# The first block of the second phase: transposed on TensorE instead of by a DMA, its rows gathered before its shares, and the renewal of two weight pieces set behind the fetch

## The chip, the cores and the metric

The kernel runs on one core of a Trainium2 chip. The metric is the time of one execution in device microseconds (us). Three executions of the kernel before took 579.71 us in the median. The profile is of one more execution.

## The reference

A linear attention (softmax of q over the head dimension, softmax of k over the sequence) feeds a mixture of eight experts, in which every token takes exactly one expert. A token takes the expert of its highest logit, or, where its local gate is 0.5 or more, the expert of the token before it.

```python
kv = np.einsum('bhsd,bhse->bhde', k_s, v)
x = np.einsum('bhsd,bhde->bhse', q_s, kv)        # 8 batches, 8 heads, 576 tokens, 64 -> rows of 512
...
for b in range(B):
    prev_e = -1
    for s in range(S):
        fresh_e = int(np.argmax(logits[b, s]))
        if s == 0 or local_gate[b, s] < 0.5:
            e = fresh_e
        else:
            e = prev_e if prev_e >= 0 else fresh_e
        prev_e = e
        ...
        h = np.maximum(x[b, s] @ w1[e], 0.0)     # 512 x 1024
        out[b, s] = p[e] * (h @ w2[e])           # 1024 x 512
```

## The kernel before

**The work.** The attention part writes the 4608 rows of x to DRAM (`xrows`) and each row's share p[e] to `shares`. The expert part then works through blocks of 128 rows of one expert. Blocks 0 to 7 are the first phase: they hold rows of the first four batches and run while the attention of the other four is still being finished. From block 8 on (`NP`, `NA` = 8) the index lists cover all rows; that is the second phase. With the inputs used, the reference's rule sends blocks 0 to 8 to expert 0, 9 to 13 to expert 2, 14 to 18 to expert 4, 19 to 23 to expert 5 and 24 to 37 to expert 7; so the weights change four times, before blocks 9, 14, 19 and 24.

**One block.** Each step has a name, and a number for the block:

- `G` (POOL) gathers the 128 rows into `xg`, four blocks ahead; `Gp` (POOL) gathers their 128 shares into `pb`.
- `Px` normalises the rows (`xn`; POOL, for blocks 8 and 10 VectorE), `Ph` makes their fp16 high part and `Pl` the low part (`x2`; ACT or DVE, and DVE).
- The rows are turned so that the 512 features lie on the partitions (`xT`). Block 0 does it with `T`, eight TensorE transposes into PSUM, and `Tc`, a VectorE copy out of it. All other blocks use `D`, a DMA transpose that SP issues.
- `F1` (PE, two halves, `.0` and `.1`) multiplies with w1 into PSUM (`ph`, `pi`); `Ac`, `Ad`, `Ar`, `Al` (ACT, DVE, ACT, DVE) make the fp16 high and low parts of the hidden values (`hi`, `lo`) of a half; `F2` (PE, two halves) multiplies with w2 (`py`, `pq`); `Gv` (ACT) scales by the share and `Pt` (POOL) scatters the rows to the output.

**The weights.** `fetch(b, 1)` and `fetch(b, 2)` are two DMAs that SP issues on a condition: they load the 2 MB of the next expert's w1 into the staging tile `s1`, of its w2 into `s2`, if block b is the first of its expert. `renew` cuts staged weights into fp16 high and low parts, in 16 pieces (0 to 7 of w1, 8 to 15 of w2), each a step on ACT and one on DVE, inside an `If` on the flag that the block begins an expert. `RN` and `s1`, `s2` are the names of these steps in the first phase.

**What sets the order.** For the attention part and blocks 0 to 7, and for the preparation of blocks 8 to 10, a text (`ORDER`) lists all steps by name; each engine runs its own steps in that order, and waits only for what a step needs. From block 8 on, `block(b)` writes the steps. Its renewals for the block after it end with pieces 8 and 9.

**The place of the change.** The stretch of `ORDER` around the end of block 7 is, on PE: `F2.7.0`, then the first step of `block(8)`, `F1.8.0` (`ffn1`, line 869, `hidden`, lines 888 and 893), then `F2.7.1` and `F1.8.1`. On SP: `s1.7` (the w1 of expert 2), `s2.7`, `s1.8`, and then `D.8`, `D.9`, `D.10` (`turn_dma`, line 866). `s1.8` may not write `s1` before the fetch of `s1.7` has landed there; its condition is false in this run, so it moves nothing. On DVE: `Px.8`, `Ph.8`, `Pl.8` (lines 845, 191, 853), `Ad.7.1` (901), `Px.10`, `Al.7.1` (908), `Pl.9`, `Ph.10`, `Pl.10`.

Of the kernel before, what the change touches and what calls it, by code (L numbers as in the profile page):

```python
# [18 lines left out]
B, H, S, D = 8, 8, 576, 64  # L19
# [12 lines left out]
NA = 8  # L32
NB = NBM - NA
NP = 8
NQE = 3
NT_PE = 1
NW = 6
NG = NE + 1
NX = 1 + NG + D
# [14 lines left out]
class Plan:  # L54
# [7 lines left out]
    def add(self, name, eng, fn, after=(), takes=(), uses=(), order=(), alt=None):  # L62


        eng = alt if name in self.swap else eng
        before = list(order) + list(uses)
        for r, _ in takes:
            if r in self.chained:
                before += [self.head[r]] if r in self.head else []
                self.head[r] = name  # L70
        self.tasks[name] = (eng, fn, list(after), list(takes), before, alt)
        for u in takes:
            self.taker[u] = name
        for u in set(uses) | set(takes):
            self.users.setdefault(u, []).append(name)
# [68 lines left out]
ro.2.0 Al.4.0 RN.4.3 bc Gv.3 s2.4 ro.3.4 bi.p0 Gp.7 bi F2.4.0 Ac.4.1 Pt.3 RN.5.1 bj.p0 ro.3.8 s1.5 Ad.4.1 ro.3.0 bj.p1 F1.5.0 RN.5.2 Ar.4.1 bj.p2  # L144
ro.3.1 Al.4.1 bj.p3 ro.3.7 F2.4.1 bj.p4 Ac.5.0 RN.6.0 Ad.5.0 ro.3.3 bj Ar.5.0 F1.5.1 bb.p0 Gv.4 RN.5.3 Pt.4 ro.3.5 s2.5 Al.5.0 ro.3.6 ro.3.2 F2.5.0
RN.6.1 bb Ac.5.1 s1.6 bo.0 Ad.5.1 bo.3 Ar.5.1 bo.1 bm.0 RN.6.2 Al.5.1 bm.1 bm.3 bo.2 F1.6.0 F2.5.1 Ac.6.0 RN.7.0 Ad.6.0 Ar.6.0 Al.6.0 F1.6.1 Gv.5
RN.6.3 Pt.5 s2.6 bm.2 Ac.6.1 F2.6.0 bx.p0 RN.7.1 s1.7 Ad.6.1 bx Ar.6.1 Gp.8 Al.6.1 F1.7.0 RN.7.2 G.8 G.9 F2.6.1 RN.8.0 Ac.7.0 G.10 Ad.7.0 G.11 Ar.7.0
F1.7.1 Al.7.0 Gv.6 RN.7.3 Px.8 Pt.6 s2.7 Ph.8 Px.9 F2.7.0 Ac.7.1 Pl.8 RN.8.1 Ph.9 s1.8 Ad.7.1 D.8 Px.10 Ar.7.1 Al.7.1 Pl.9 D.9 Ph.10 Pl.10 D.10
"""


# [1 line left out]
def moe_kernel(ctx, tc, q, k, v, w_gate, w_local, w1, w2, out, dbg=None):  # L153
# [23 lines left out]
    def at(pair, b):  # L177

        return pair[0][:, b] if b < NA else pair[1][:, b - NA]
# [647 lines left out]
    def word(w_, hi_, engines):  # L827
        return nc.values_load(w_, min_val=0, max_val=hi_, engines=engines,
                              skip_runtime_bounds_check_because="clamped where it is worked out")

    def gather(b):
        src = xrows[0:2 * 1152, :] if b < NA else xrows
        i_, j_ = (gidx[0], b) if b < NA else (gidx[1], b - NA)
        nc.gpsimd.indirect_dma_start(out=xg[b % AHEAD], out_offset=None, in_=src,  # L834
                                     in_offset=bass.IndirectOffsetOnAxis(ap=i_[:, j_:j_ + 1], axis=0))

    def gather_share(b):
        src = shares[0:2 * 1152, :] if b < NA else shares
        i_, j_ = (gidx[0], b) if b < NA else (gidx[1], b - NA)
        nc.gpsimd.indirect_dma_start(out=pb[b % NPB], out_offset=None, in_=src,  # L840
                                     in_offset=bass.IndirectOffsetOnAxis(ap=i_[:, j_:j_ + 1], axis=0))
# [121 lines left out]
    def renew(b, pieces):  # L963
        with tc.If(fst[b] == 1):  # L964
            for i in pieces:
                cut_hi(i, nc.scalar)
                cut_lo(i, nc.vector)
# [6 lines left out]
    def fetch(b, i):  # L974

        if b >= NBM - 1:
            return
        s_, src = ((W["s1"], w1_src), (W["s2"], w2_src))[i - 1]
        w_ = at(info, b)
        cond, e = w_[:, 4:5], w_[:, 1:2]  # L980
        if b == NA - 1:
            cond = None if i == 1 else w_[:, 0:1]
        elif b == NA - 2 and i == 2:
            cond, e = w_[:, 2:3], w_[:, 3:4]
        kw = {} if cond is None else dict(cond=(word(cond, 1, [ET.SP]) == 1), cond_hint=False)
        nc.sync.dma_start(out=s_, in_=src(bass.ds(word(e, NE - 1, [ET.SP]), 1)), **kw)
# [4 lines left out]
    add, split = pl.add, pl.split  # L991
    plan.append(pl)
    PE, DVE, ACT, POOL, SP = "PE", "DVE", "ACT", "Pool", "SP"
# [88 lines left out]
    for b in range(NP + 4):  # L1082
        add(("G", b), POOL, gather, after=[("ax",) if b < NA else ("bx",)] + [("xs", t, u) for t in range(2 if b < NA else NTILE) for u in range(3)],
            order=[("ow",)], takes=[("xg", b)])
        if b <= NP:
            add(("Gp", b), POOL, gather_share, after=[("ax",) if b < NA else ("bx",)] + [("Sd", t) for t in range(1 if b < NA else 2)],
                order=[("ow",)], takes=[("pb", b)])
        if b >= NP + 3:
            continue
        add(("Px", b), POOL, prep_x, alt=DVE, after=[("G", b)], uses=[("xg", b)], takes=[("xn", b)])  # L1090
        add(("Ph", b), ACT, prep_hi, alt=DVE, after=[("Px", b)], uses=[("xn", b)], takes=[("x2", b)])
        add(("Pl", b), DVE, prep_lo, after=[("Ph", b)], uses=[("xn", b), ("x2", b)])
        if b < NT_PE:
            add(("T", b), PE, turn, after=[("Pl", b)], takes=[("pst", b)], uses=[("x2", b)])
            add(("Tc", b), DVE, turn_copy, after=[("T", b)], uses=[("pst", b)], takes=[("xT", b)])
        else:
            add(("D", b), SP, turn_dma, after=[("Pl", b)], uses=[("x2", b)], takes=[("xT", b)])
        if b > NP:
            continue
        if b > 0:  # L1100
            for i in range(2 if b == NP else 4):
                src = [("F1", b - 1, 0), ("F1", b - 1, 1), ("F2", b - 1, 0), ("F2", b - 1, 1)][i]
                add(("RN", b, i), ACT, renew4, after=[src, ("aj",) if b < NA else ("bj",)], order=[("s1" if i < 2 else "s2", b - 1)])
            add(("s1", b), SP, lambda b: fetch(b, 1), after=[("RN", b, 1)] + ([("bj",)] if b >= NA - 1 else []))
        else:
            add(("s1", b), SP, lambda b: fetch(b, 1), after=[("Wl", i) for i in range(8)] + [("aj",)], order=[("W", 3)])
        if b == NP:
            continue
        add(("s2", b), SP, lambda b: fetch(b, 2),
            after=([("RN", b, 3)] if b else [("Wl", i) for i in range(8, 16)] + [("aj",)]) + ([("bj",)] if b >= NA - 2 else []))  # L1110
        for g in range(2):
            wp_ = [("Wl", 4 * g + i) for i in range(4)] if b == 0 else [("RN", b, g)]
            add(("F1", b, g), PE, ffn1, after=[("Tc" if b < NT_PE else "D", b)] + wp_, order=[("ow",)] + ([("F2", b - 1, g)] if b else [("F1", 0, 0)] * g)
                + ([("F1", b, 0)] if g else []), takes=[("psh", (b, g))], uses=[("xT", b)])
            add(("Ac", b, g), ACT, act_copy, after=[("F1", b, g)], uses=[("psh", (b, g))], takes=[("hf", (b, g))])
            add(("Ad", b, g), DVE, act_add, after=[("Ac", b, g)], uses=[("psh", (b, g)), ("hf", (b, g))])
            add(("Ar", b, g), ACT, act_hi, after=[("Ad", b, g)], uses=[("hf", (b, g))] + ([("hh", b)] if g else []), takes=[] if g else [("hh", b)])
            add(("Al", b, g), DVE, act_lo, after=[("Ar", b, g)], uses=[("hf", (b, g)), ("hh", b)])
            if b == NP - 1 and g:
                continue  # L1120
            wp_ = [("Wl", 8 + 4 * g + i) for i in range(4)] if b == 0 else [("RN", b, 2 + g)]
            add(("F2", b, g), PE, ffn2, after=[("Al", b, g)] + wp_, order=[("F1", b, 1)] if g == 0 else [("F1", b + 1, 0)],
                takes=[] if g else [("psy", b)], uses=[("hh", b)] + ([("psy", b)] if g else []))
        if b < NP - 1:
            add(("Gv", b), ACT, give, after=[("F2", b, 1), ("Gp", b)], uses=[("psy", b), ("pb", b)], takes=[("y", b)])
            add(("Pt", b), POOL, put, after=[("Gv", b)], uses=[("y", b)])
# [3 lines left out]
    def prep_a(b):  # L1130
        if b < NBM:
            prep_x(b)
# [12 lines left out]
    def next_(b, pieces):  # L1145
        if b + 1 < NBM:
            renew(b + 1, pieces)

    def block(b):


        if b + AHEAD < NBM:
            gather(b + AHEAD)
        prep_a(b + 3)
        if b + 1 < NBM:
            gather_share(b + 1)
            if b + 1 not in fst:
                flag(b + 1)
        ffn1(b, 0)
        act(b, 0)  # L1160
        renew(b, FROM[b][0])
        next_(b, (0, 1))
        ffn2(b - 1, 1)
        ffn1(b, 1)
        give(b - 1)
        put(b - 1)
        renew(b, FROM[b][1])
        next_(b, (2, 3))
        prep_b(b + 3)
        act(b, 1)  # L1170
        renew(b, FROM[b][2])
        next_(b, (4, 5, 6, 7))
        ffn2(b, 0)
        next_(b, (8, 9))
        if b + 3 < NBM:
            turn_dma(b + 3)
        fetch(b, 2)
        if b + 1 < NBM:
            fetch(b + 1, 1)


    FROM = {b: ((10, 11), (12, 13), (14, 15)) for b in range(NBM)}
# [50 lines left out]
```

## Time and profile before

| | |
|---|---|
| median of three executions | 579.71 us (576.01 to 580.80) |
| the profiled execution | 581.13 us |
| its span, first to last instruction | 579.4 us |
| TensorE busy, share of the span | 86% |
| mean granted TensorE clock, share of 2.4 GHz | 0.946 |

The span is 1.7 us shorter than the profiled execution's own time, and that execution is 1.4 us above the median. A sum made in the trace is therefore taken off 581.13 us, and then 1.4 us more are taken off to compare it with the median.

### The profile page before, as it was taken

What the parts mean: (1) busy time and instruction counts of PE and PEld (TensorE: products, weight loads), DVE (VectorE), ACT (ScalarE), POOL (GpSimd) and SP (SyncE); (2) the same over time, 40 slices, a digit from 0 to 9 for tenths busy, and PEclk for the clock granted to TensorE, in tenths of its full rate; (3) what the DMA queues carried; (4) which work ended last, traced back from release to release, by engine and by line L of the source; (5) the groups of instructions that cost most, each with busy time, mean ns of one, the idle gap of its engine ahead of it and who ended that gap; (6) DMA issues with size and microseconds to landing.
All of it is one profiled execution on the core that took longest, in us unless ns stands there. A gap on an engine that the chain in (4) does not pass through costs nothing. (4 is left out here: it accounts for less than half of the span.)

```text
span 579.4 us, 16087 instructions
## 1 busy us (share of the span) xinstructions
PE 500.4 (86%) x6074; PEld 353.1 (61%) x6074; DVE 344.3 (59%) x651; ACT 267.5 (46%) x454; POOL 231.1 (40%) x239
## 2 busy tenths in 40 slices
PE   1677677665799999859999899999998999999995
PEld 0556556554666767546666566766666667766762
DVE  5978999997775784428535833674386333333331
ACT  2625557566533283217335633654374333333332
POOL 3551528525345111514535335334445253352431
PEclk9877899986799999969999999999999999999999
DMA  9999695639546202934973794279559934242351
GB/s 307 384 381 384 219 307 202 230 125 359 181 89 155 58 20 48 381 79 115 302 109 99 203 213 104 75 207 207 105 106 297 115 94 82 61 116 61 82 95 48
DMA packets 80435, 98.59 MB, mean 170 GB/s; under 512 B 47679, under 2 KB 55871, under 8 KB 80320
## 3 DMA queue, kind: packets, MB, share of 16 engines
q1 hardware_dynamic: 72672, 74.92, 45.8%
q0 software_dynamic: 7648, 22.20, 14.4%
q8 instruction: 65, 1.06, 0.8%
q14 instruction: 50, 0.41, 0.3%
HBM read 206.76 MB, written 20.89 MB: 393 GB/s over the span
## 5 line engine op out<-in xcount | busy, mean ns | idle before, releaser
L926 POOL DMA_INDIRECT out<-y,sidx x38 | 39.0, 1027 | 201.0 <-ACTq L964 160.6
L888 PEld LDWEIGHTS <-w1h 128*128 128x128 f16 x1216 | 104.6, 99 | 15.4 <-issue 0.8
L888 PE MATMUL ph<-xT,w1h 128*128 128x256 f16 (+1 forms) x640 | 101.4, 272 | 11.5 <-DMA xT<-x 8.8
L893 PEld LDWEIGHTS <-w1l 128*128 128x128 f16 x1216 | 91.8, 98 | 26.5 <-issue 12.4
L919 PEld LDWEIGHTS <-hi 128*128 128x128 f16 x608 | 58.9, 98 | 61.8 <-ACT hi L904 6.2
L888 PE MATMUL pi<-xT,w1h 128*128 128x256 f16 (+1 forms) x576 | 89.2, 268 | 0.0
L908 DVE SCALAR_TENSOR_TENSOR lo<-hf,hi 128x512 f16<-128x512 f32 x76 | 55.3, 728 | 44.7 <-ACTq L964 36.5
L904 ACT ACTIVATE hi<-hf 128x512 f16<-128x512 f32 x76 | 47.8, 629 | 71.6 <-DVE hf L901 69.9
L901 DVE TENSOR_TENSOR hf<-ph,hf 128x512 f32<-128x512 f32 x40 | 27.6, 691 | 75.2 <-ACT hf L898 63.4
L919 PE MATMUL py<-w2h,lo 128*128 128x512 f16 x184 | 69.8, 379 | 1.6 <-DVEq L964 1.2
L919 PE MATMUL py<-w2h,hi 128*128 128x512 f16 x184 | 69.8, 379 | 1.4 <-ACT hi L904 1.4
L919 PE MATMUL py<-w2l,hi 128*128 128x512 f16 x184 | 69.7, 379 | 0.0
L898 ACT COPY hf<-ph 128x512 f32<-128x512 f32 x40 | 23.4, 584 | 93.0 <-PE ph L888 85.9
L893 PE MATMUL ph<-xT,w1l 128*128 128x128 f16 (+1 forms) x640 | 61.9, 219 | 0.5 <-issue 0.5
L853 DVE SCALAR_TENSOR_TENSOR x<-xn,x 128x512 f16<-128x512 f32 x41 | 34.6, 845 | 38.4 <-ACT x L187 36.9
L840 POOL DMA_INDIRECT pb<-shares,gidx x39 | 42.7, 1095 | 35.0 <-ACTq L964 12.5
L834 POOL DMA_INDIRECT xg<-xrows,gidx x42 | 47.1, 1121 | 21.1 <-issue 11.1
L919 PEld LDWEIGHTS <-lo 128*128 128x128 f16 x304 | 29.9, 98 | 41.3 <-DVE lo L908 3.5
L893 PE MATMUL pi<-xT,w1l 128*128 128x128 f16 (+1 forms) x576 | 54.4, 217 | 0.0
L919 PE MATMUL pq<-w2h,hi 128*128 128x512 f16 x120 | 46.3, 385 | 3.7 <-ACT hi L904 3.7
L919 PE MATMUL pq<-w2h,lo 128*128 128x512 f16 x120 | 46.1, 384 | 0.3
L919 PE MATMUL pq<-w2l,hi 128*128 128x512 f16 x120 | 46.2, 385 | 0.0
(227 smaller groups left out, 754.6 us busy)
## 6 DMA issues: line engine op xcount, KB each, us to landing
s<-in_moe_w SPq DMA_DIRECT2D x77, 2048.0 KB
xrows<-xt SPq DMA_DIRECT2D x12, 888.0 KB
KT<-in_k SPq DMA_DIRECT2D x16, 576.0 KB
VT<-in_v SPq DMA_DIRECT2D x16, 576.0 KB
qt<-in_q SPq DMA_DIRECT2D x8, 640.0 KB
qt<-in_q SPq DMA_DIRECT2D x8, 512.0 KB
s<-in_moe_w SPq DMA_DIRECT2D x4, 1024.0 KB
xg<-xrows,gidx POOLq DMA_INDIRECT x42
```

Source lines behind the costliest of these rows:

```text
L834: nc.gpsimd.indirect_dma_start(out=xg[b % AHEAD], out_offset=None, in_=src, in_offset=bass.IndirectOffsetOnAxis(ap=i_[:, j_:j_ + 1], axis=0))
L840: nc.gpsimd.indirect_dma_start(out=pb[b % NPB], out_offset=None, in_=src, in_offset=bass.IndirectOffsetOnAxis(ap=i_[:, j_:j_ + 1], axis=0))
L853: nc.vector.scalar_tensor_tensor(out=x2[b % 2][:, 1, :], in0=xn[b % 2], scalar=XS, in1=x2[b % 2][:, 0, :], op0=ALU.mult, op1=ALU.subtract)
L888: nc.tensor.matmul(ph_[:, f, :].rearrange("p (i t) -> p i t", i=2)[:, :, 0:n], W["w1h"][:, c, fs], xT_[:, :, c, 0:n], start=(c == 0), stop ...
L893: nc.tensor.matmul(ph_[:, f, 0:n], W["w1l"][:, c, fs], xT_[:, 0, c, 0:n], start=False, stop=False)
L898: nc.scalar.copy(hf[g], phs[g][:, :, P:2 * P])
L901: nc.vector.tensor_tensor(out=hf[g], in0=phs[g][:, :, 0:P], in1=hf[g], op=ALU.add)
L904: nc.scalar.activation(hi[b % 2][:, 4 * g:4 * g + 4, :], hf[g], AF.Relu)
L908: nc.vector.scalar_tensor_tensor(out=lo[b % 2][:, gs_, :], in0=hf[g], scalar=0.0, in1=hi[b % 2][:, gs_, :], op0=ALU.max, op1=ALU.subtract)
L919: nc.tensor.matmul(result(b), h_[:, f, :], w_[:, f, :], start=(f == 0 and i == 0), stop=(f == 7 and i == 2))
L926: nc.gpsimd.indirect_dma_start(out=outr, out_offset=bass.IndirectOffsetOnAxis(ap=i_[:, j_:j_ + 1], axis=0), in_=ys[b % 2], in_offset=None, ...
```

## The change

Three things change. First, block 8 (`NA`) is turned as block 0 is, by `T.8` on PE and `Tc.8` on DVE, and `D.8` is gone; `T.8` stands behind `F2.7.0`, `Tc.8` ahead of `Ad.7.1`. Second, `G.8` and `Gp.8` change places on POOL. Third, in `block(b)` the renewal of pieces 8 and 9 for the next block is written behind `turn_dma` and both fetches, not ahead of them. In the old order, if a block is the only one of its expert, pieces 8 and 9 of the next are cut from `s2` before their weights are fetched; no expert has a single block after block 8 in this run.

```diff
-NT_PE = 1
...
-... bx Ar.6.1 Gp.8 Al.6.1 F1.7.0 RN.7.2 G.8 G.9 F2.6.1 RN.8.0 ...
+... bx Ar.6.1 G.8 Al.6.1 F1.7.0 RN.7.2 Gp.8 G.9 F2.6.1 RN.8.0 ...
-... F2.7.0 Ac.7.1 Pl.8 RN.8.1 Ph.9 s1.8 Ad.7.1 D.8 Px.10 Ar.7.1 Al.7.1 Pl.9 D.9 ...
+... F2.7.0 Ac.7.1 Pl.8 T.8 RN.8.1 Ph.9 s1.8 Tc.8 Ad.7.1 Px.10 Ar.7.1 Al.7.1 Pl.9 D.9 ...
...
-        if b < NT_PE:
+        if b in (0, NA):
             add(("T", b), PE, turn, after=[("Pl", b)], takes=[("pst", b)], uses=[("x2", b)])
             add(("Tc", b), DVE, turn_copy, after=[("T", b)], uses=[("pst", b)], takes=[("xT", b)])
         else:
...
         ffn2(b, 0)
-        next_(b, (8, 9))
         if b + 3 < NBM:
             turn_dma(b + 3)
         fetch(b, 2)
         if b + 1 < NBM:
             fetch(b + 1, 1)
+        next_(b, (8, 9))
```

On PE, between the last matmul of `F2.7.0` and the first of `F1.8.0` (`x_2057` is block 8's `x2`, `pt` the PSUM tile, `xT_2059` block 8's `xT`), before:

```order
L919 LDWEIGHTS lo_2078
L919 MATMUL py_2068<-w2h,lo_2078 128x512
L828 TENSOR_LOAD info_78
L875 COMPARE_AND_BRANCH
L888 LDWEIGHTS w1h
L888 MATMUL ph_2083<-xT_2059,w1h 128x2x64
```

and now, with one line number less throughout, since a line at the top is gone:

```order
L918 LDWEIGHTS lo_2078
L918 MATMUL py_2068<-w2h,lo_2078 128x512
L859 LDWEIGHTS x_2057
L859 MATMUL pt_2067<-id_67,x_2057 128x128
L827 TENSOR_LOAD info_78
L874 COMPARE_AND_BRANCH
L887 LDWEIGHTS w1h
L887 MATMUL ph_2083<-xT_2059,w1h 128x2x64
```

The pair of L859 rows stands there eight times, for four blocks of columns of two parts. On DVE, from behind `Pl.8` to the first step of block 8 (`hf_2080` is written by `Ad.7.1`, `lo_2078` by `Al.7.1`, `x_2058` by `Pl.9`, `x_2057` by `Ph.10` and `Pl.10`), before:

```order
L901 TENSOR_TENSOR hf_2080<-pi_2896,hf_2080 128x512
L845 TENSOR_TENSOR xn_2055<-xg_2053 128x512
L908 SCALAR_TENSOR_TENSOR lo_2078<-hf_2080,hi_2076 128x512
L853 SCALAR_TENSOR_TENSOR x_2058<-xn_2056,x_2058 128x512
L875 UNCONDITIONAL_BRANCH
L191 TENSOR_SCALAR x_2057<-xn_2055 128x512
L853 SCALAR_TENSOR_TENSOR x_2057<-xn_2055,x_2057 128x512
```

and now:

```order
L862 COPY xT_2059<-pt_2067 128x1024
L900 TENSOR_TENSOR hf_2080<-pi_2896,hf_2080 128x512
L874 UNCONDITIONAL_BRANCH
L844 TENSOR_TENSOR xn_2055<-xg_2053 128x512
L907 SCALAR_TENSOR_TENSOR lo_2078<-hf_2080,hi_2076 128x512
L852 SCALAR_TENSOR_TENSOR x_2058<-xn_2056,x_2058 128x512
L190 TENSOR_SCALAR x_2057<-xn_2055 128x512
L852 SCALAR_TENSOR_TENSOR x_2057<-xn_2055,x_2057 128x512
```

The copy `Tc.8` is new and stands ahead of everything that finishes block 7; the rest keeps its order. On SP, from `s1.8` (`s_2036` is `s1`) on, before:

```order
L986 ISA
L986 DMA s_2036<-in_moe_w 128x4x1024
L866 DMA_TRANSPOSE xT_2059<-x_2057 128x8x128
L866 DMA_TRANSPOSE xT_2060<-x_2058 128x8x128
L875 UNCONDITIONAL_BRANCH
L866 DMA_TRANSPOSE xT_2061<-x_2057 128x8x128
```

and now:

```order
L985 ISA
L985 DMA s_2036<-in_moe_w 128x4x1024
L874 UNCONDITIONAL_BRANCH
L865 DMA_TRANSPOSE xT_2060<-x_2058 128x8x128
L865 DMA_TRANSPOSE xT_2061<-x_2057 128x8x128
```

`D.8` is gone from behind `s1.8`; `D.9` and `D.10` stay behind it.

## Rows read from the trace of the kernel before

**Rows 1.** The page, span in 40 slices: TensorE clock granted, tenths of full speed.

```profile
PEclk9877899986799999969999999999999999999999
```

**Rows 2.** Stretches: length; busy us (count) of PE, PEld, DVE, ACT, POOL; PEclk; DMA share; GB/s.

```profile
226.00:243.50 17.50, 17.50 (x148) 11.68 (x147) 7.27 (x16) 5.02 (x8) 6.80 (x7) 1.00 0.82 289
243.50:252.30 8.80, 0.02 (x2) 0.01 (x1) 2.30 (x4) 1.15 (x2) 4.07 (x4) 0.69 0.68 193
252.30:257.20 4.90, 4.90 (x32) 4.02 (x32) 1.12 (x2) 0.00 (x0) 0.00 (x0) 0.52 0.31 61
257.20:275.50 18.30, 18.30 (x147) 12.09 (x145) 13.49 (x22) 13.72 (x25) 6.47 (x6) 1.00 0.34 98
```

**Rows 3.** Waits of PE from 200 to 580 us: total, times, longest.

```profile
PE ph L888 <- DMA xT<-x: 8.8, 1, 8.8
PE pq L919 <- ACT hi L904: 3.7, 2, 1.8
```

**Rows 4.** Timeline of PE: start, us, work [idle before it, what ended that].

```profile
232.73 0.27 PE L888 MATMUL ph<-xT,w1h 128*128 128x256 f16 x1
...
235.37 0.38 PE L919 MATMUL py<-w2h,hi 128*128 128x512 f16 x1
...
243.13 0.38 PE L919 MATMUL py<-w2h,lo 128*128 128x512 f16 x1
...
252.29 0.37 PE L888 MATMUL ph<-xT,w1h 128*128 128x256 f16 x1 [8.78 <-DMA xT<-x]
...
257.21 0.38 PE L919 MATMUL py<-w2h,hi 128*128 128x512 f16 x1
```

**Rows 5.** Timeline of SP's queue, the issue of `D.8`.

```profile
248.56 1.29 SPq L866 DMA_TRANSPOSE xT<-x  x1
```

**Rows 6.** Waits of SP's queue from 240 to 252 us.

```profile
SPq L986 <- DMA s<-in_moe_w: 6.6, 1, 6.6
```

**Rows 7.** Timeline of DVE: `Px.8`, `Pl.8`, `Ad.7.1`, `Px.10`.

```profile
241.04 0.69 DVE L845 TENSOR_TENSOR xn<-xg 128x512 f32<-128x512 f32 x1 [1.24 <-DMA xg<-xrows,gidx]
...
242.29 0.69 DVE L853 SCALAR_TENSOR_TENSOR x<-xn,x 128x512 f16<-128x512 f32 x1
...
243.12 0.69 DVE L901 TENSOR_TENSOR hf<-pi,hf 128x512 f32<-128x512 f32 x1
...
245.25 0.69 DVE L845 TENSOR_TENSOR xn<-xg 128x512 f32<-128x512 f32 x1 [1.44 <-DMA xg<-xrows,gidx]
```

**Rows 8.** Timeline of block 0, which is turned on PE: `T.0`, `Tc.0`, `F1.0.0`.

```profile
151.72 0.61 PE L860 MATMUL pt<-id,x 128*128 128x128 f16 x8
...
153.19 0.69 DVE L863 COPY xT<-pt 128x1024 f16<-128x1024 f16 x1
...
153.93 0.27 PE L888 MATMUL ph<-xT,w1h 128*128 128x256 f16 x1 [0.91 <-DVE xT L863]
```

**Rows 9.** Stretch around `Tc.0` (columns as in Rows 2).

```profile
152.00:154.00 2.00, 1.09 (x39) 0.92 (x37) 1.65 (x4) 2.00 (x5) 0.00 (x0) 1.00 0.29 111
```

**Rows 10.** Timeline of block 9: `Pl.12` on DVE, `Px.12` on POOL, `F2.9.1` on PE.

```profile
275.36 2.26 DVE L853 SCALAR_TENSOR_TENSOR x<-xn,x 128x512 f16<-128x512 f32 x1 [0.23 <-ACT x L187]
...
275.99 1.07 POOL L845 TENSOR_TENSOR xn<-xg 128x512 f32<-128x512 f32 x1
...
278.94 0.39 PE L919 MATMUL py<-w2h,hi 128*128 128x512 f16 x1 [0.65 <-ACT hi L904]
```

**Rows 11.** Timeline of blocks 8 and 9: pieces 8 and 9 on ACT, `Al.9.0`, `F2.9.0`.

```profile
267.65 1.13 ACT L187 ACTIVATE w2h<-s 128x512 f16<-128x512 f32 x2
...
271.39 0.69 DVE L908 SCALAR_TENSOR_TENSOR lo<-hf,hi 128x512 f16<-128x512 f32 x1 [0.70 <-ACT hi L904]
...
272.90 0.38 PE L919 MATMUL py<-w2h,hi 128*128 128x512 f16 x1
```

**Rows 12.** SP's queue on line 986, 264 to 271 us: `fetch(8, 2)`, its wait and its issue.

```profile
L986 SPq EVENT_SEMAPHORE  x1: 3019/3019/3019, 267.1 to 267.1; - x1
...
L986 SPq DMA_DIRECT2D s<-in_moe_w x1: 80/80/80, 270.2 to 270.2; - x1
```

More of the change, by code (lines that the diff above doesn't have):

```diff
@@ L146 @@
 RN.6.1 bb Ac.5.1 s1.6 bo.0 Ad.5.1 bo.3 Ar.5.1 bo.1 bm.0 RN.6.2 Al.5.1 bm.1 bm.3 bo.2 F1.6.0 F2.5.1 Ac.6.0 RN.7.0 Ad.6.0 Ar.6.0 Al.6.0 F1.6.1 Gv.5
-RN.6.3 Pt.5 s2.6 bm.2 Ac.6.1 F2.6.0 bx.p0 RN.7.1 s1.7 Ad.6.1 bx Ar.6.1 Gp.8 Al.6.1 F1.7.0 RN.7.2 G.8 G.9 F2.6.1 RN.8.0 Ac.7.0 G.10 Ad.7.0 G.11 Ar.7.0
-F1.7.1 Al.7.0 Gv.6 RN.7.3 Px.8 Pt.6 s2.7 Ph.8 Px.9 F2.7.0 Ac.7.1 Pl.8 RN.8.1 Ph.9 s1.8 Ad.7.1 D.8 Px.10 Ar.7.1 Al.7.1 Pl.9 D.9 Ph.10 Pl.10 D.10
+RN.6.3 Pt.5 s2.6 bm.2 Ac.6.1 F2.6.0 bx.p0 RN.7.1 s1.7 Ad.6.1 bx Ar.6.1 G.8 Al.6.1 F1.7.0 RN.7.2 Gp.8 G.9 F2.6.1 RN.8.0 Ac.7.0 G.10 Ad.7.0 G.11 Ar.7.0
+F1.7.1 Al.7.0 Gv.6 RN.7.3 Px.8 Pt.6 s2.7 Ph.8 Px.9 F2.7.0 Ac.7.1 Pl.8 T.8 RN.8.1 Ph.9 s1.8 Tc.8 Ad.7.1 Px.10 Ar.7.1 Al.7.1 Pl.9 D.9 Ph.10 Pl.10 D.10
 """
@@ L1112, in moe_kernel @@
             wp_ = [("Wl", 4 * g + i) for i in range(4)] if b == 0 else [("RN", b, g)]
-            add(("F1", b, g), PE, ffn1, after=[("Tc" if b < NT_PE else "D", b)] + wp_, order=[("ow",)] + ([("F2", b - 1, g)] if b else [("F1", 0, 0)] * g)
+            add(("F1", b, g), PE, ffn1, after=[("Tc" if b in (0, NA) else "D", b)] + wp_, order=[("ow",)] + ([("F2", b - 1, g)] if b else [("F1", 0, 0)] * g)
                 + ([("F1", b, 0)] if g else []), takes=[("psh", (b, g))], uses=[("xT", b)])
```

## The prediction

> **What bounds the kernel now.** I began with the page's 40 slices [rows 1]. After the attention part the granted TensorE clock is full in nearly every slice; one slice, the 18th (246 to 261 us), shows 6 tenths. Cutting the place into stretches [rows 2] gives the reason: up to 243.5 us PE is busy all the time at clock 1.00, then for 8.8 us it does next to nothing, then it works for 4.9 us at 0.52, and after that it is busy without a gap at 1.00. So the second phase is a chain of matmuls with one hole at its start. The waits of PE [rows 3] name what ends it: one wait of 8.8 us for the DMA that writes `xT`. The next in that list is 3.7 us, two waits for `hi`. What starts block 8 later starts everything after it later.
>
> Next comes the question why that DMA came late. On PE the last matmul of `F2.7.0` starts at 243.13 and ends at 243.51, and `F1.8.0` starts at 252.29 [rows 4]. Its input `x2` is done much earlier: `Pl.8` runs from 242.29 to 242.98 [rows 7]. But `D.8` is issued at 248.56 only [rows 5], and in front of it on SP's queue stands `s1.8`, which waited 6.6 us for an earlier fetch into the same staging tile [rows 6]. So of the 9.3 us from `Pl.8` to `F1.8.0`, 5.6 are the queue in front of `D.8` and 3.7 (252.29 less 248.56) the transpose itself.
>
> **The turn of block 8 on PE.** This takes `D.8` off the path, and with it SP's queue. `F2.7.0` ends at 243.51, and the input of `T.8` has then been ready for 0.5 us. The eight transposes of `T.0` took 0.61 us together [rows 8]; `T.8` then ends at 244.12. The copy `Tc.0` took 0.69, and `F1.0.0` started 0.05 us after it (153.93 less 153.88); I take as much for the hand-over from PE to DVE. `F1.8.0` then starts at 244.12 + 0.05 + 0.69 + 0.05 = 244.91. Before it started at 252.29: 7.38 us are gained.
>
> Then the clock. Half a block's `F1` at full clock took 235.37 - 232.73 = 2.64 us; `F1.8.0` took 257.21 - 252.29 = 4.92 us [rows 4], since during the 8.8 us without matmuls the clock had fallen, and the half ran at 0.52, nearly all of it at the lower level of 1.2 GHz [rows 2]. In the new order PE lacks work for 244.91 - 244.12 = 0.8 us. Beside `Tc.0` it lacked work for 0.91 us, a little after the same eight transposes [rows 8], and the clock in that stretch is 1.00 [rows 9]. So I take full clock: 2.28 us more. The sum is 9.66 us.
>
> The Trainium skill, "TensorE: Matmul & The Clock Gate", Part 4 (PE-mode transpose), speaks against this: transposes do not count as TensorE being busy in the way that matmuls do, so `T.8` might not help to hold the clock. The stretch of `Tc.0` speaks against the rule, though not by itself, for 32 small matmuls stood between those transposes and the wait; by the rule the 2.28 us would be lost, and the sum be 7.38.
>
> **What is queued behind the new steps.** `Tc.8` makes DVE wait for PE until 244.17, and `Ad.7.1`, which ran at 243.12 [rows 7], now starts at 244.9, 1.8 us later. Who waits for that? `Ar.7.1` and `Al.7.1`, for `F2.7.1`. `Ad.7.1` ends at 245.5; then `Px.10`, whose rows were there at 245.25 [rows 7], until 246.2; `Ar.7.1` runs on ACT meanwhile; `Al.7.1` until 246.9. `F2.7.1` can start at 244.91 + 2.64 = 247.55. The cover is 0.6 us, so I cost it at nothing; if the gathers come that much later, the excess is paid once, up to some 1 us.
>
> **What is late next.** Nothing on SP: `D.9` takes `D.8`'s place at 248.56, is there by about 252.3 if it takes `D.8`'s 3.7 us, and `F1.9.0` starts three halves of some 2.6 us behind the start of `F2.7.1`, at about 255.3. The w1 of expert 2 is in `s1` when `s1.8` is let go, before 248.56; ACT can cut the first piece only behind `Ar.8.0`, which follows the end of `F1.8.0` (247.5) by three steps of some 0.7 us, so not before 249.5. On DVE there is one doubt. `Pl.9`, `Ph.10` and `Pl.10` were done while PE stood still; now they fall into the first matmuls of block 8, beside `Px.11` on POOL. In block 9 the same pair met, and `Pl.12` took 2.26 us instead of 0.69, after which PE waited 0.65 us for `hi` [rows 7, 10]. That prices a meeting at block 8: 1.57 us on DVE, of which PE feels between nothing and 1 us. The Trainium skill, "SBUF — State Buffer", section "SBUF: two separate sides", has the rule behind it: a VectorE instruction with two SBUF inputs and a GpSimd instruction that reads SBUF exclude each other, and the later one blocks for the whole instruction. The trace agrees. I take zero in the sum and 1 us in the range.
>
> **Rows before shares.** `G.8` goes ahead of `Gp.8`. What it can give is the 1.24 us that `Px.8` waited for its rows [rows 7]; then `Pl.8` ends at 241.7. But `T.8` waits for `F2.7.0` until 243.51, so this is worth nothing here; it makes the cover of `T.8` 1.8 us instead of 0.5. The shares are first used by `Gv.8`, a whole block later. Zero; at worst the later gathers shift by less than the 0.6 us above.
>
> **The two pieces.** `next_` behind the fetches leaves the steps of ACT and DVE as they were, but pieces 8 and 9 now wait for `fetch(b, 2)`, in four blocks (8, 13, 18, 23). In none of them is b the first of its expert, so that fetch moves nothing: its issue took 80 ns [rows 12]. It used to wait for these two pieces, from 267.1 to 270.1, having all else [rows 12]; now it can go at about 267.2. ACT wants piece 8 at 267.65 [rows 11]: 0.4 us of cover. Behind the pieces on ACT stands `Ac.9.0`, and PE waits for what comes of it at `F2.9.0`: `Al.9.0` ends at 272.08, `F2.9.0` starts at 272.90 [rows 11], another 0.8 us. Zero, and if SP came 2 us late, 0.8 us at each of four places. The other side is bounded too: `fetch(9, 1)` goes some 2 us earlier, but it is needed five blocks later, so no gain.
>
> **Sum.** 581.13 - 9.66 = 571.47 us for the profiled execution; that one lies 1.42 us above the median, so the median becomes 570.05, in round numbers 570.0.
>
> **The rivals.**
>
> (a) The hole is closed, but part of it opens again in blocks 8 and 9: DVE and ACT have lost the pause in which they caught up. For it: the meeting on DVE and the thin covers of 0.6 and 0.8 us. Against it: PE had no gap from 257.2 to 275.5 [rows 2], with the same steps relative to `F1.8.0`, and only three more steps on DVE to carry. Price: 1.6 us on DVE in block 8 and as much again in block 9, with a fall of the clock behind one of them (2.3): 2 to 5 us, 572 to 575, say 573.
>
> (b) The clock falls all the same: PE has only the transposes between 243.51 and 244.91, and `F1.8.0` runs at the lower level as it did before. Price 2.28 us: 572.3. Against it: the clock beside `Tc.0` [rows 9]. It is what the rule of the Trainium skill on PE-mode transposes, named above, would give.
>
> (c) The change does not reach the hole: some other input of `F1.8.0` is as late as the DMA was. The wait then stays near 8.8 us under another name, and the time near 580. Against it: the profile names the DMA as what ended the wait, the weights of block 8 are those of block 7, and its PSUM tile was read by `Ad.7.0`, a step before `Px.8` on DVE.
>
> (d) Slower. The wait for `fetch(b, 2)` is a real one. It decides if, in a block before a change of expert, that fetch is taken: then ACT and DVE stand before piece 8 until 2 MB have landed. At the 289 GB/s of the first stretch [rows 2] that is 7.3 us; less the covers of 0.4 and 0.8, PE loses 6.1 us, and 2.3 more by the clock, at four places: 33.6 us against a gain of 9.7, so 604. Below 2.4 us a place it would not outweigh the gain. Against it: the 80 ns, and 30 blocks of five experts of which none has a single block.
>
> **How the numbers follow.** The forecast, 570.0, has a chance of 0.68 with its own range of 567.5 to 572.5. (a) has 0.14, (b) 0.06, (c) 0.08, (d) 0.04. A measurement of this kernel can tell about 1% from no change, 5.8 us: faster than 573.9. The forecast and (b) lie below that, and so do seven tenths of (a): 0.68 + 0.06 + 0.10 = 0.84 faster; 0.04 of (a) and (c) give 0.12 within 1%; (d) 0.04 slower. The three executions of before span 4.8 us, 3.7 below and 1.1 above their median. So the range goes from 566.5 (the forecast and such a low run) to 574.5 (the costly half of (a)); (c), (d) and the tails are left out.
>
> **What would show it.** In the changed kernel's trace: eight transposes right behind `F2.7.0`, a second copy from `pt` of 0.69 us, `F1.8.0` less than 1 us behind the transposes, the clock 1.00 from 240 to 260 us, no wait of PE for the DMA into `xT`, 39 DMA transposes instead of 40, and blocks as long as before (`F1` to `F1` 10.5 us). The forecast is wrong if PE waits for `hi` or `lo` at `F2.7.1`, `F2.8.0` or `F2.8.1` for more than 1 us, or if ACT stands before piece 8 of the weights.

## The result

| | before | after |
|---|---|---|
| median of four executions each | 578.85 us (576.01 to 580.80) | 571.37 us (570.12 to 572.15) |
| ratio of the times on record, 95% interval | | 0.9873 (0.9824 to 0.9921) |
| the profiled execution, its span | 581.13, 579.4 us | 570.12, 568.4 us |
| mean granted TensorE clock | 0.946 | 0.965 |

The change makes the kernel 1.3% faster, by 7.5 us; the forecast was 570.0 us, in a range of 566.5 to 574.5. A few executions of the experiments ran in a slower state of the chip, and the medians below leave them out.

The clock by 40 slices, from the page of the kernel after; the 18th slice, 6 tenths in [rows 1], is now at 9 (the 10th lies in the attention part and is at 6 in both):

```profile
PEclk9988899896899999999999899999999999999999
```

Stretches of the kernel after, with the columns of [rows 2]: block 7, the transposes and the pause behind them, `F1.8.0`, and block 8 with most of block 9:

```profile
223.00:240.60 17.60, 17.60 (x150) 11.80 (x148) 7.18 (x15) 5.02 (x8) 7.62 (x8) 1.00 0.78 281
240.60:242.03 1.43, 0.65 (x10) 0.49 (x8) 0.75 (x2) 0.63 (x1) 1.24 (x2) 1.00 1.01 397
242.03:244.66 2.63, 2.63 (x32) 2.45 (x32) 2.53 (x5) 0.63 (x1) 0.00 (x0) 1.00 0.75 273
244.66:265.70 21.04, 21.04 (x178) 14.44 (x175) 17.09 (x24) 13.91 (x25) 10.68 (x10) 1.00 0.63 186
```

Where [rows 2] had 8.80 us with PE at work for 0.02, there are now 1.43 us with PE at work for 0.65, and the clock is 1.00 in all four stretches. The waits of PE from 200 us on, in the kernel after:

```profile
PE pq L918 <- ACT hi L903: 3.7, 2, 1.8
PE py L918 <- ACT hi L903: 2.1, 2, 1.4
PE ph L887 <- DVE xT L862: 0.8, 1, 0.8
```

The 8.8 us for the DMA of [rows 3] have become 0.8 us for the copy on DVE. What heads the list now are the waits for `hi`, which were second before. The start of `F2.7.0` in the kernel before, which [rows 4] leaves out:

```profile
240.76 0.38 PE L919 MATMUL py<-w2h,hi 128*128 128x512 f16 x1
```

The same place in the kernel after, step by step, the timeline of PE (start, us, work, idle before it):

```profile
238.05 0.38 PE L918 MATMUL py<-w2h,hi 128*128 128x512 f16 x1
...
240.42 0.38 PE L918 MATMUL py<-w2h,lo 128*128 128x512 f16 x1
240.64 0.61 PE L859 MATMUL pt<-id,x 128*128 128x128 f16 x8
242.03 0.27 PE L887 MATMUL ph<-xT,w1h 128*128 128x256 f16 x1 [0.78 <-DVE xT L862]
...
244.66 0.38 PE L918 MATMUL py<-w2h,hi 128*128 128x512 f16 x1
```

From the start of `F2.7.0` to that of `F2.7.1` it is 244.66 - 238.05 = 6.61 us; before it was 257.21 [rows 4] less 240.76, so 16.45. The transition has become 9.84 us shorter. On DVE, and on POOL where it meets DVE, the timeline of the same stretch shows:

```profile
237.27 0.69 DVE L844 TENSOR_TENSOR xn<-xg 128x512 f32<-128x512 f32 x1 [0.15 <-DMA xg<-xrows,gidx]
...
238.46 0.69 DVE L852 SCALAR_TENSOR_TENSOR x<-xn,x 128x512 f16<-128x512 f32 x1
...
241.28 0.69 DVE L862 COPY xT<-pt 128x1024 f16<-128x1024 f16 x1 [2.13 <-PE pt L859]
241.89 0.68 DVE L900 TENSOR_TENSOR hf<-pi,hf 128x512 f32<-128x512 f32 x1
...
244.70 1.11 POOL L844 TENSOR_TENSOR xn<-xg 128x512 f32<-128x512 f32 x1 [2.71 <-DVE x L852]
244.94 1.42 DVE L852 SCALAR_TENSOR_TENSOR x<-xn,x 128x512 f16<-128x512 f32 x1
```

`Px.8` hardly waits for its rows here (0.15 us, 1.24 in [rows 7]; the experiments show that this wait differs from execution to execution) and `Pl.8` is done at 239.15, 1.5 us before `T.8` can start; `Ad.7.1` follows the copy at once; `Pl.10` meets the `Px.11` of POOL and takes 1.42 us. PE feels nothing of that in block 8. In block 9, from the timeline of the kernel after:

```profile
263.54 2.26 DVE L852 SCALAR_TENSOR_TENSOR x<-xn,x 128x512 f16<-128x512 f32 x1 [0.23 <-ACT x L186]
264.18 1.06 POOL L844 TENSOR_TENSOR xn<-xg 128x512 f32<-128x512 f32 x1
...
267.11 0.39 PE L918 MATMUL py<-w2h,hi 128*128 128x512 f16 x1 [1.37 <-ACT hi L903]
```

These answer to [rows 10]: `Pl.12` is as long as it was, and PE's wait at `F2.9.1` has grown from 0.65 to 1.37 us, so that 0.72 us are given back. (The `Px` on POOL beside `Pl.12` is that of the following block, `Px.13`, not `Px.12` as the heading of [rows 10] has it: `Px.12` must be over before `Pl.12` can begin.)

From the start of `F2.7.1` to the last matmul's end it is 316.4 us after and 315.7 before, so nothing else of the second phase moved up to there; in both traces the clock fell once, behind a pause in block 14, of which the last section tells. The two profiled executions are 11.0 us apart. The rest of that is the execution and not the change: before was 2.7 us later already at the start of `F2.7.0` (240.76 against 238.05; the first repeat of the changed kernel has 240.75 there), and behind the last matmul it needed 0.9 us less (6.5 against 7.3; the repeat needed 6.5).

### The profile page after: what moved, and what is told of

Same layout as the page of the kernel before. It is cut to its first block, busy times and chain, and to the rows that moved or that the text cites. A ratio compares the mean times of both kernels' runs of the same rounds, so it can differ in the third digit from the quotient of the medians.

```text
span 568.4 us, 16132 instructions
## 1 busy us (share of the span) xinstructions
PE 494.3 (87%) x6082; PEld 348.9 (61%) x6082; DVE 342.5 (60%) x652; ACT 267.6 (47%) x454; POOL 232.5 (41%) x239
## 5 line engine op out<-in xcount | busy, mean ns | idle before, releaser
L887 PE MATMUL ph<-xT,w1h 128*128 128x256 f16 (+1 forms) x640 | 99.7, 269 | 3.4 <-DVE xT L862 1.8
```

The costliest lines, as they stand in the source:

```text
L887: nc.tensor.matmul(ph_[:, f, :].rearrange("p (i t) -> p i t", i=2)[:, :, 0:n], W["w1h"][:, c, fs], xT_[:, :, c, 0:n], start=(c == 0), stop ...
```

## The experiments

Twelve runs, in three groups of four; each group ran on one chip beside runs of the kernel before on that chip, and times of one group are compared with each other only. The interval behind a ratio is the 95% one. The ratio is the one on record; it is not the quotient of the two medians and differs from it by up to 0.2%.

### The parts, each alone

The changed kernel once more gives the yardstick of the first group.

> The changed kernel itself once more, as the yardstick for the runs beside it. If the gain is the closed hole of the second phase, about 9 us against one execution of before whose hole is as long as the profiled one: a ratio of 0.984 to 0.988, 569 to 572 us. If the first four runs of each kernel were only luckily spread, nearer 0.990.

Measured: 572.34 us, before 579.97; 0.9859 (0.9809 to 0.9908).

The turn alone: `T.8` and `Tc.8` as in the change, the other two edits taken back.

```diff
-... G.8 Al.6.1 F1.7.0 RN.7.2 Gp.8 G.9 ...
+... Gp.8 Al.6.1 F1.7.0 RN.7.2 G.8 G.9 ...
...
+        next_(b, (8, 9))
         if b + 3 < NBM:
             turn_dma(b + 3)
         fetch(b, 2)
         if b + 1 < NBM:
             fetch(b + 1, 1)
-        next_(b, (8, 9))
```

> The turn of block 8 on PE alone: shares again gathered ahead of rows, and the two weight pieces again ahead of the fetches. Theory of the prediction (the turn is the whole gain, the two reorderings are worth nothing): the time of the full change within 1 us, 570 to 572 us, F1.8.0 less than 1 us behind the transposes; the transposes start at once behind F2.7.0. Rival (the rows have to come first for the transposes to be in time): Px.8 waits 1.2 us or more for its rows again, T.8 starts 0.5 us or more after F2.7.0 ends, and 1 to 2 us are lost: 572 to 574 us. Rival (the order of fetch and pieces carries part of it): SP waits some 3 us for the pieces in blocks 8, 13, 18, 23, and the time is longer by whatever of that reaches PE.

Measured: 571.93 us, 0.9846 (0.9798 to 0.9894): the whole gain, with PE's wait of 0.78 us before `F1.8.0` and 1.37 before `F2.9.1` as in the full change. SP stood before `fetch(8, 2)` again, from the SP queue's rows on that line:

```profile
L985 SPq EVENT_SEMAPHORE  x1: 2967/2967/2967, 257.3 to 257.3; - x1
```

Nothing waits for SP there, so those 3.0 us cost nothing. From the start of `F2.7.0` to the end of the last matmul it is 323.1 us, against 323.0 in the full change.

This trace does not test the first rival: `Px.8` waits for no rows in it, although the shares are gathered first again. Three other traces can tell, of kernels with the old order of the gathers (36 matmuls, 128 transposes, and the last run of all, below). There `Px.8` waits 2.5 to 2.8 us, and `Pl.8` is still done 0.2 to 0.5 us before `F2.7.0` ends. So the transposes would have been in time there too, by less than in the full change.

The two reorderings alone: the kernel before with the diff of the run above read the other way round, and `D.8` in its old place.

> The two reorderings without the turn: block 8 is again turned by a DMA that stands behind the conditional fetch of w1 on SP. Theory of the prediction: as before, 577 to 581 us, with PE's wait of 8 to 9 us for the DMA into xT, since SP stands in the fetch whether the rows come early or late. Rival (the rows were what was late): the wait shrinks by the 1.2 us that Px.8 waited for its rows, and 1 to 2 us are gained: 577 us or less.

Measured: 580.97 us against 579.97, 0.9997 (0.9966 to 1.0028). `Px.8` does not wait for its rows, and yet PE's list begins as it did before:

```profile
PE ph L888 <- DMA xT<-x: 8.1, 1, 8.1
```

So the turn is the whole gain, and the two reorderings together are worth nothing that the times can tell, with the turn and without it; neither was run alone. In this one trace the wait is 0.7 us shorter than in [rows 3], and `F1.8.0` took 4.02 us instead of 4.92. Whether the order of the gathers did that or the execution stays open.

### What the late DMA was made of

The kernel before with `D.8`, still a DMA, ahead of `s1.8` on SP:

```diff
-... Pl.8 RN.8.1 Ph.9 s1.8 Ad.7.1 D.8 Px.10 ...
+... Pl.8 D.8 RN.8.1 Ph.9 s1.8 Ad.7.1 Px.10 ...
```

> The kernel before with one step moved: D.8, still a DMA transpose, stands on SP ahead of the conditional fetch s1.8 instead of behind it. This parts the 9.3 us from Pl.8 to F1.8.0 into queue and transpose. Theory of the prediction (5.6 us queue, 3.7 us transpose): D.8 is issued within 0.5 us of the end of Pl.8, F1.8.0 starts 3.7 to 4.2 us after Pl.8's end, PE waits 3.2 to 4 us instead of 8.8, and the kernel gains 5 to 6 us, up to 2.3 more if the clock does not fall in so short a wait: 571 to 575 us. Rival (the transpose is slow because of the 2 MB fetch that moves beside it, and waits for it wherever it stands in the queue): D.8 lands when the fetch has landed, near the old time, and the kernel is as before, 578 to 580 us.

Measured: 576.84 us against 579.97, 0.9961 (0.9928 to 0.9993): 2 to 3 us gained where 5 to 6 or more were expected. SP's queue and PE in this kernel's timeline:

```profile
242.07 1.40 SPq L866 DMA_TRANSPOSE xT<-x  x1
247.45 0.09 SPq L986 DMA_DIRECT2D s<-in_moe_w  x1
...
248.36 0.37 PE L888 MATMUL ph<-xT,w1h 128*128 128x256 f16 x1 [5.85 <-DMA xT<-x]
```

`D.8` is issued 0.1 us after the end of `Pl.8` (241.29 + 0.69), as the theory has it. But from its issue to `F1.8.0` it is 6.29 us, not 3.7. `s1.8`, which waits for the 2 MB of `s1.7`, is let go at 247.45, and `F1.8.0` starts 0.91 us after that. So the transposed block is there only when the fetch ahead of it has landed: of the 5.6 us by which `D.8` now goes earlier, 2.9 shorten the hole (8.78 less 5.85) and 2.7 have become a wait in the DMA. `F1.8.0` took 4.23 us, 0.7 less than before. Each theory holds a part. The Trainium skill, "DMA: Bandwidth & Descriptors", section "Queues, rings and completion order", says that each DMA engine takes what one issuing engine sends it in order, and that a transfer's semaphore comes only after that engine's earlier writes; these rows agree with it. They cannot tell that order from two transfers that merely share the DMA engines.

### The clock by itself, and whether transposes hold it

Two kernels keep the hole of the kernel before and fill it with work on PE that nobody reads, ahead of `F1.8.0`: 36 matmuls, or 128 transposes.

```diff
+        if b == NP:
+            for i in range(36):
+                nc.tensor.matmul(py[1], W["w1h"][:, 0, 0:P], W["w2h"][:, 0, :], start=True, stop=True)
         ffn1(b, 0)
```

```diff
+        if b == NP:
+            for i in range(128):
+                nc.tensor.transpose(pt[0][:, i % 2, i // 2 % 4, :], id16, id16)
         ffn1(b, 0)
```

> The kernel before, with 36 matmuls of 128x512 whose result nobody reads put on PE between F2.7.0 and F1.8.0. They take 0.22 us each, some 7.8 us, so that the hole of 8 to 9 us stays as long as it was and only PE's idleness in it goes. This prices the clock by itself. Theory of the prediction (F1.8.0 is slow only because the clock fell in the hole): F1.8.0 takes 2.6 to 2.8 us instead of 4.7 to 4.9, and the kernel gains 2 us: 577 to 579 us beside 580. Rival (F1.8.0 is slow for another reason, its weights or xT arriving late): it still takes over 4 us at clock 1.00.

> As the run with 36 matmuls in the hole, but with 128 transposes of the identity instead, some 0.06 us each, 7.3 us in all. This tests the rival of the prediction by which transposes do not hold the clock (the Trainium skill, "TensorE: Matmul & The Clock Gate", Part 4). Theory of the prediction: the clock is 1.00 through the transposes, F1.8.0 takes 2.6 to 2.8 us, and the gain is that of the matmuls, 2 us. Rival: the clock falls during the transposes as it falls in the empty hole, they take longer than 0.06 us each towards the end, and F1.8.0 takes over 4 us; the kernel is then as before or up to 3 us slower.

Measured, beside 572.52 us of before on that chip: 570.75 with matmuls, 0.9988 (0.9954 to 1.0022), and 569.93 with transposes, 0.9965 (0.9933 to 0.9996). Gains of 2 us are near what these intervals can tell, so the traces decide. Stretches of the kernel with matmuls: the matmuls, the rest of the hole, `F1.8.0`:

```profile
235.30:243.23 7.93, 7.93 (x37) 3.52 (x36) 2.46 (x4) 1.15 (x2) 4.07 (x4) 1.00 0.62 202
243.23:244.56 1.33, 0.00 (x0) 0.00 (x0) 0.00 (x0) 0.00 (x0) 0.00 (x0) 1.00 1.04 199
244.56:247.18 2.62, 2.62 (x32) 2.45 (x32) 1.12 (x2) 0.00 (x0) 0.00 (x0) 1.00 0.12 23
```

The same three of the kernel with transposes:

```profile
238.03:245.34 7.31, 7.31 (x129) 7.13 (x127) 2.60 (x4) 1.15 (x2) 4.06 (x4) 1.00 0.95 232
245.34:246.92 1.58, 0.00 (x0) 0.10 (x1) 0.00 (x0) 0.00 (x0) 0.00 (x0) 1.00 0.48 75
246.92:249.56 2.64, 2.64 (x32) 2.46 (x32) 1.12 (x2) 0.00 (x0) 0.00 (x0) 1.00 0.10 19
```

In both the hole is as long as ever, and `F1.8.0` takes 2.62 and 2.64 us, at clock 1.00, instead of 4.92. So the slow `F1.8.0` was the clock and nothing else, and transposes hold the clock here as matmuls do: 7.3 us of nothing else, a pause of 1.58 us, and still 1.00. The rule by which transposes do not count as TensorE being busy in the way that matmuls do (the Trainium skill, "TensorE: Matmul & The Clock Gate", Part 4) does not show in this kernel.

Then the other side, a longer pause in the changed kernel: `Tc.8` done three times.

```diff
-        nc.vector.tensor_copy(out=xT[b % 4], in_=pt[0])
+        for _ in range(3 if b == NA else 1):
+            nc.vector.tensor_copy(out=xT[b % 4], in_=pt[0])
```

> The changed kernel with Tc.8 done three times over, so that two copies of 0.69 us are added between the transposes and F1.8.0. Theory of the prediction (Tc.8 is on the path, and the cover of Ad.7.1 moves with it): PE waits 2.16 us instead of 0.78 before F1.8.0, F2.7.1 follows without a wait of its own, and 1.4 us are lost if the clock holds, up to 3.7 if it falls: 0.2 to 0.6% above the changed kernel, hardly to be told by the times, so read in the trace. Rival (F1.8.0 has another input almost as late, or the rest of block 7 on VectorE becomes the bound): the wait grows by less than 1.2 us, or PE waits a second time at F2.7.1 for lo.

Measured: 566.61 us, 0.9878 (0.9836 to 0.9921) of before, 1.8 us above the changed kernel on that chip (564.78). Its stretches are the pause behind the transposes and `F1.8.0`:

```profile
236.11:238.34 2.23, 0.00 (x1) 0.00 (x0) 2.12 (x4) 0.63 (x1) 1.26 (x2) 1.00 0.92 352
238.34:242.63 4.29, 4.29 (x32) 3.58 (x32) 4.16 (x6) 0.63 (x1) 1.47 (x2) 0.60 0.34 100
```

The pause grew from 0.78 to 2.23 us, by the two copies, so `Tc.8` is on the path. PE waited for nothing at `F2.7.1`: the cover of `Ad.7.1` moves with the copy. And behind a pause of 2.23 us the clock did fall: `F1.8.0` took 4.29 us at 0.60, most of it at 1.2 GHz, 1.66 more than in the changed kernel. Here PE waited only 0.65 us at `F2.9.1`, so 0.7 of the 3.1 us (1.45 of pause and 1.66 of clock) came back there.

### The waits that the change leaves

What heads PE's list in the changed kernel are waits for `hi` at the second half of the first block of each new expert, behind a `Pl` of 2.26 us beside a `Px` on POOL. Two edits of the changed kernel were made against that meeting. In the first, `Px` runs on VectorE from block 11 on:

```diff
-    eng = on("Px", b) if ("Px", b) in plan[0].tasks else nc.gpsimd
+    eng = on("Px", b) if ("Px", b) in plan[0].tasks else nc.vector
```

In the second it stays on POOL, behind the gather of the shares:

```diff
-        prep_a(b + 3)
         if b + 1 < NBM:
             gather_share(b + 1)
+        prep_a(b + 3)
```

> The changed kernel with one more edit: from block 11 on Px (rows times their scale) runs on VectorE instead of POOL, at the same place of the block. What is left of PE's waits behind the change are 1.37, 1.83, 0.77 and 1.83 us at the second half of the first block of a new expert, each behind a Pl of 2.26 us that ran beside a Px on POOL. Theory (the meeting of Pl and Px is the cause): Pl takes 0.69 everywhere, those four waits fall under 0.5 us each, and 4 to 7 us are gained, 0.987 to 0.993 of the changed kernel. Rival (VectorE has too much work in those blocks, whoever slows it): 0.69 us more a block on it in front of Ad keeps the waits, or moves them to the first half, and the time is the same or 1 to 3 us longer.

> The changed kernel with Px left on POOL but set behind the gather of the shares in each block from 8 on, about 1.4 us later. In block 9 of the changed kernel Px begins 0.64 us after Pl and Pl then takes 2.26 us; 1.4 us later Pl, at 0.69, is over. Theory (the meeting is the cause, and it hangs on when both start): the four waits fall under 0.7 us each, 3 to 7 us are gained. Rival: Px meets the next VectorE instruction with two SBUF inputs instead (Al or a piece of the weights), which is lengthened in the same way, and the waits stay within 0.5 us: no change.

Measured beside 572.52 us of before: 559.29 us, 0.9793 (0.9751 to 0.9835), with `Px` on VectorE; 565.67 us, 0.9895 (0.9863 to 0.9927), with `Px` later. The first kernel's block 9 in its timeline, with VectorE's two steps and PE's wait:

```profile
259.23 0.69 DVE L852 SCALAR_TENSOR_TENSOR x<-xn,x 128x512 f16<-128x512 f32 x1 [0.23 <-DVEq L963]
259.83 0.69 DVE L900 TENSOR_TENSOR hf<-pi,hf 128x512 f32<-128x512 f32 x1
...
261.24 0.39 PE L918 MATMUL py<-w2h,hi 128*128 128x512 f16 x1 [0.27 <-ACT hi L903]
```

And the second's:

```profile
259.15 0.69 DVE L852 SCALAR_TENSOR_TENSOR x<-xn,x 128x512 f16<-128x512 f32 x1 [0.23 <-ACT x L186]
...
261.04 1.05 POOL L844 TENSOR_TENSOR xn<-xg 128x512 f32<-128x512 f32 x1
261.14 1.51 DVE L907 SCALAR_TENSOR_TENSOR lo<-hf,hi 128x512 f16<-128x512 f32 x1 [0.70 <-ACT hi L903]
...
262.71 0.39 PE L918 MATMUL py<-w2h,lo 128*128 128x512 f16 x1 [0.94 <-DVE lo L907]
```

`Pl` takes 0.69 us in both. On VectorE `Px` is out of the way, and the wait falls to 0.27 us. Later on POOL it meets `Al`, which then takes 1.51 us, and PE waits 0.94 us for `lo` instead. That is the rival of this run. The changed kernel did not run on this chip, so the traces are compared: from the start of `F1.8.0` to the end of the last matmul this kernel needs 319.4 us, the changed kernel 319.0 and its first repeat 317.5. Nothing is gained, and the theory that it hangs on when both start falls, since there is another instruction to meet at either time. With `Px` on VectorE the same stretch is 313.3 us.

The last group ran the changed kernel, `Px` on VectorE in the changed kernel a second time, and the same edit in the kernel before.

> The changed kernel again, as the yardstick on the same chip for the runs with Px on VectorE and with three copies. 0.983 to 0.990 of before.

> The changed kernel with Px on VectorE from block 11 on, a second time, now beside the changed kernel itself. By the first run's trace PE keeps no wait of over 0.4 us behind block 8, where the changed kernel has 5.8 us of such waits. Theory: 5 to 7 us below the changed kernel, so 0.973 to 0.981 of before, 0.988 to 0.992 of the changed kernel. Rival: the first run's low time was mostly its chip and its attention part; then 2 us or less below the changed kernel.

> The kernel before, with Px on VectorE from block 11 on and nothing else: block 8 is still turned by a DMA. It asks whether the two gains add up. Theory (the hole at block 8 and the meetings of Pl and Px are two things): the hole of 8 to 9 us and the slow F1.8.0 stay, the later waits of 0.65, 1.83, 0.77 and 1.83 us go: 4 to 7 us gained, 0.988 to 0.993 of before. Rival (the waits at the new experts were there because block 8 began late or early): they stay, and the time is that of before.

Measured beside 573.63 us of before: the changed kernel 564.78, 0.9842 (0.9801 to 0.9882); with `Px` on VectorE 558.90, 0.9747 (0.9708 to 0.9787); the kernel before with `Px` on VectorE 566.31 (four executions), 0.9873 (0.9821 to 0.9925). PE's waits from 200 us on, with `Px` on VectorE in the changed kernel:

```profile
PE pq L918 <- ACT hi L903: 1.2, 4, 0.3
PE ph L887 <- DVE xT L862: 0.8, 1, 0.8
PE py L918 <- ACT hi L903: 0.3, 1, 0.3
```

In the kernel before with the same edit:

```profile
PE ph L888 <- DMA xT<-x: 8.7, 1, 8.7
PE pq L919 <- ACT hi L904: 1.2, 4, 0.4
```

The hole at block 8 stays where only `Px` is moved, the waits for `hi` shrink to 1.5 and 1.2 us, and the two gains add up as far as can be told. By the times they are 8.9 and 7.3 us alone and 14.7 together, each known to 2 or 3 us. The traces are sharper: from the start of `F2.7.0` to the end of the last matmul it is 332.2 us before, 323.0 with the change, 326.6 with `Px` moved, and 317.2 with both, so 9.2 and 5.6 us alone and 14.9 together. Some 1.6 us of what moving `Px` gives is the clock: it fell behind the pause in block 14 in the first two of these traces, as the last section tells, and in the other two that pause is down to 0.3 us and the clock stays at 1.00. The version with both is the fastest kernel of this study, 2.5% below the kernel before and 1.0% below the changed one.

## Why the prediction held, step by step

- **The bound.** Right. The second phase was a chain of matmuls with one hole, and closing it moved everything behind it by the same amount, but for 0.7 us at block 9.
- **The turn on PE.** Right: from the last matmul of `F2.7.0` to `F1.8.0` it took 1.61 us, forecast 1.78 (244.91 less 243.13).
- **The clock.** Right in this kernel: `F1.8.0` took 2.63 us, forecast 2.64. The filled holes show the cause, and that transposes hold the clock, so rival (b) falls. The price of 2.28 us is that of one execution: behind empty holes `F1.8.0` took 4.02 to 5.07 us, so 1.4 to 2.4 more than at full clock. And the argument did not know where the margin ends: pauses of 0.78 to 1.58 us held the clock, those of 1.83 us sometimes (the last section tells of them), and the one of 2.23 us did not.
- **The sum.** 9.66 us forecast, 9.84 measured in the transition of the two traces. By the medians of three groups of runs the change gave 7.5, 7.6 and 8.9 us, with intervals some 5 us wide. The 9.2 us of the traces (9.84 less 0.67 behind `F2.7.1`) lie within all three; the times alone cannot tell them from 7.5. That 570.0 came within 1.4 us of the measured median is in part luck, given such noise.
- **Why the DMA was late.** Incomplete, without harm to the sum. The split of 9.3 us into 5.6 of queue and 3.7 of transpose is what the trace shows, but the two parts are not independent, although the expectation for `D.8` ahead of `s1.8` took them to be. Issued earlier it took 6.3, while the fetch was still moving. The 3.7 us were the price of a transpose behind a fetch that had landed. The sum needed only that all of it goes.
- **What is queued behind.** Right: no wait at `F2.7.1`, even with the copy done three times.
- **Rows before shares, and the two pieces.** Right: the two together are worth zero, from both sides. The 1.24 us that `Px.8` waited were one execution's; over the traces it is 0 to 2.8 us in the old order and 0 to 1.7 in the new, and the cover of `T.8` was never used up. In the kernel after, SP issued `fetch(8, 2)` at 255.33, and ACT began piece 8 at 255.82, behind the last piece of w1, without a wait: 0.5 us of cover against the 0.4 that the prediction had.
- **The doubt on DVE.** Half right. `Pl.10` met `Px.11`, and the price was 0.73 us (1.42 less 0.69), not 1.57. PE paid 0.72 us, inside the 0 to 1 us of the range, but one block later than thought, at `F2.9.1`. In the kernel before, VectorE and ACT seem to have had a lead from the hole or the slow `F1.8.0`: where the hole was kept, with a full clock, the wait was 0.64 or 0.65 us, and with the hole closed but `F1.8.0` slow it was 0.65; with neither it was 1.37 (1.36 to 1.37 in four traces). So rival (a) came true, at less than half of its lowest price of 2 us.
- **Rivals (c) and (d).** Both fall: the wait on the DMA is gone, and the fetch of those four blocks is not taken.

## What to carry to other kernels

When an engine waits for a DMA, look at what else is in that queue before you move the issue. Here a transfer set ahead of a waiting step still landed behind the bulk transfer that was issued before it, and another path (PE and VectorE) took it off. A hole on TensorE cost its length and then the slow stretch behind it; count both, and price the pause that is left by the nearest pauses in the traces on either side. After a hole is closed, read the list of waits again: the next ones here, 5.8 us where two elementwise engines met, fell to 1.5 us when one small step was moved from the one to the other.

## What the runs showed of the hardware that was not expected

**The same pause, two outcomes.** At the second half of block 14 PE pauses for 1.82 or 1.83 us in ten of the traces, those of before and after among them. Behind it the clock fell in five of them and not in the other five. The stretch of the pause and the 3.4 us behind it, in the kernel after:

```profile
317.54:319.37 1.83, 0.00 (x1) 0.01 (x1) 1.13 (x3) 0.69 (x2) 1.25 (x1) 1.00 0.36 135
319.37:322.77 3.40, 3.28 (x9) 1.14 (x10) 2.55 (x4) 1.57 (x3) 0.00 (x0) 0.60 0.47 90
```

In the same kernel's first repeat:

```profile
320.22:322.05 1.83, 0.00 (x1) 0.00 (x1) 1.13 (x3) 0.68 (x2) 1.26 (x1) 1.00 0.37 135
322.05:325.45 3.40, 3.28 (x19) 1.58 (x20) 2.55 (x4) 1.57 (x3) 0.00 (x0) 1.00 0.44 88
```

The work before the pause is the same; 9 matmuls were begun behind it in the one case, 19 in the other. From `F2.14.1` to PE's wait in block 19 it is 55.2 us (319.37 to 374.53) where the clock fell and 53.5 us (322.05 to 375.58) where it did not, so this one pause makes 1.6 us of difference between two executions of one kernel. The same ten traces have a second pause of 1.83 us, at the second half of block 24 (426.77 in the kernel after), and behind that one the clock stayed at 1.00 in all ten. So the length of the pause alone does not decide it. What does stays open.

**Who pays for a meeting.** Where a VectorE instruction with two SBUF inputs and POOL's `Px` overlapped, VectorE's became longer (0.69 to 1.42, 1.51 or 2.26 us) and POOL's stayed at 1.05 to 1.11. In all three rows shown above VectorE ends 0.55 or 0.56 us behind POOL's end (246.36 and 245.81; 262.65 and 262.09; 265.80 and 265.24), as if it did most of its work only then. That holds in block 9 too, where `Pl` is recorded as the earlier by 0.64 us; so the prediction's word that the trace agrees with the rule of the Trainium skill is too strong. The lengthening fits a rule by which the two exclude each other; that the later one yields does not fit the recorded starts.
